# The numerator of a rational function in SBUF instead of PSUM, in the first half of an MoE layer

## The chip, the cores and the metric

The kernel runs on one core of a Trainium2 chip. The metric is the device time of one execution in microseconds. TensorE is called PE, VectorE DVE, ScalarE ACT, GpSimd POOL and SyncE SP, as in the profile. All times of the kernel before are from three timed runs and from one profiled execution.

## What is computed

Three layers follow each other: a pooled attention, a first MoE layer whose activation is a rational function, and a second MoE layer with routing over all tokens. The change is in the activation of the first MoE. Cut to that:

```python
x = attention(q, k, v)               # 4608 tokens x 512
h = x @ w_in                         # 4608 x 2048
P = a[0] + a[1]*h + a[2]*h*h + a[3]*h*h*h
Q = 1.0 + abs(b[0])*abs(h) + abs(b[1])*h*h
g = P / (Q + 1e-06)
x = g @ w_out                        # 4608 x 512, then the second MoE
```

## The kernel before, in words

The 4608 tokens are 18 blocks of 256. The 2048 hidden features are two halves of 1024 (`half` 0 and 1), each of four pieces of 256 (`fp` 0 to 3). The kernel passes over all blocks with the first half, then over all blocks with the second, then does the routing and the second MoE. Attention is computed in the same stretch as the first half: its scores (line 560), transposes (595) and products with v (613 to 616) stand between the matmuls of the first half until about 500 us.

The unit of work is a step: 512 columns of h, either one block times two chunks of 128 features or two blocks times one chunk. There are 72 steps in each half. One step is:

- `mm_h` (line 701): 24 matmuls of 256 columns or 12 of 512 write h into one PSUM bank, `ph`. Each product is done in three parts, high and low halves of both factors.
- `act1`: ACT writes |h| to `ms` (716), a3\*h + a2 to `mw` (717) and |b1|\*|h| + |b0| to `mq` (719). In the tables `mw` and `mq` also appear as `mwq`, since two of the three buffers of each share a tile. DVE multiplies `mw` by h (721) and then computes (mw + a1)\*h (722), which it writes over h in the PSUM bank. POOL multiplies `mq` by `ms` (by way of helper line 353).
- `act2`: ACT takes the logarithm of the denominator (734) and the exponential (736), which gives 1/Q in `mr`. DVE computes the high part of g, `hi` = (numerator + a0)\*`mr` (737), then two more passes (739 and 741) that give the remainder of the division in `mt`. Lines 737 and 741 read the numerator; line 739 reads `mq` and `hi`. POOL multiplies `mt` by `mr` (353), which gives the low part, `lo`. The tiles of `hi` and `lo` are named `mg`, `mgx` or `gd`, and `woh`, `wol` and so on where spent weight tiles are used again.
- `mm_y`: PE multiplies `hi` by the high and low parts of w_out (805, 806) and, later, `lo` by the high part (803). The results of a block gather in two PSUM banks and are read out at 832.

There are eight PSUM banks of 512 columns. `ph`, the output banks, the scores, transposes and v products of attention and the preparation of weights all draw on the same eight. `mw` and `mq` are rings of three, `ms` of two.

The order of the work is not written by hand. Each operation is recorded with an engine, an estimated cost, the keys it reads and those it writes (`op`, and `either` for work that two engines can do). `Order.run` then plans: it walks the engines in the order of planned time, takes the ready operation of lowest priority number, gives a bank to the first user of a `Dyn` from those planned free, and takes it back when the last operation that uses it is planned to end. The result is one fixed instruction order for each engine, in which an instruction waits on semaphores for what it needs. While planned time is under 105 us, the planner also fills planned gaps of PE with matmuls on a tile of zeros (line 339). The bank of `ph` is held from the first matmul of a step to line 741, the last reader of the numerator.

Of the kernel before, what the change touches and what calls it, by code (L numbers as in the profile page):

```python
# [18 lines left out]
ALU = mybir.AluOpType  # L19
# [4 lines left out]
B, H, S, D = 8, 8, 576, 64  # L24
# [7 lines left out]
NB = NT // BLK  # L32
# [266 lines left out]
class Kern:  # L299
# [408 lines left out]
    def act1(self, st):  # L708

        nc, op, i = self.nc, self.op, st["i"]  # L710
        ph = st["ph"]
        hk = [(ph, 0)]
        w, q, s = self.mw[i % 3], self.mq[i % 3], self.ms[i % 2]
        st["w"], st["q"] = ph, q
        N = 2 * BLK
        op("Act", c_act(N), lambda: nc.scalar.activation(s(), ph(), AF.Abs), r=hk, w=[s])  # L716
        op("Act", c_act(N, 0, 2), lambda: nc.scalar.activation(w(), ph(), AF.Identity, scale=self.a3(), bias=self.a2()),
           r=hk + self.sk, w=[w])
        op("Act", c_act(N, 1, 2), lambda: nc.scalar.activation(q(), s(), AF.Identity, scale=self.b1a(), bias=self.b0a()),  # L719
           r=[s] + self.sk, w=[q])  # L720
        op("DVE", c_tt(N), lambda: nc.vector.tensor_tensor(w(), w(), ph(), op=ALU.mult), r=hk, w=[w])
        op("DVE", c_stt(N), lambda: nc.vector.scalar_tensor_tensor(
            ph(), w(), self.a1(), ph(), op0=ALU.add, op1=ALU.mult), r=[w], w=hk)
        self.tt(N, q, q, s, ALU.mult, r=[s], w=[q])

    def act2(self, st):

        nc, op, i = self.nc, self.op, st["i"]
        w, q, r, t = st["w"], st["q"], self.mr[i % len(self.mr)], self.mt[i % MTB]
        hi, lo = g = self.mgl.pop(0)  # L730
        self.mgl.append(g)
        st["hi"], st["lo"] = hi, lo
        N = 2 * BLK
        op("Act", c_act(N, 1, 1), lambda: nc.scalar.activation(r(), q(), AF.Ln, scale=2.0 ** -LNS, bias=self.qcs()),
           r=[q], w=[r])
        op("Act", c_act(N, 1, 1), lambda: nc.scalar.activation(r(), r(), AF.Exp, scale=-1.0, bias=self.nls()), w=[r])
        op("DVE", c_stt(N), lambda: nc.vector.scalar_tensor_tensor(hi(), w(), self.a0(), r(), op0=ALU.add, op1=ALU.mult),  # L737
           r=[(w, 0), r], w=[hi])
        op("DVE", c_stt(N), lambda: nc.vector.scalar_tensor_tensor(t(), q(), self.qc(), hi(), op0=ALU.add, op1=ALU.mult),
           r=[q, hi], w=[t])  # L740
        op("DVE", c_stt(N), lambda: nc.vector.scalar_tensor_tensor(  # L741
            t(), w(), self.a0(), t(), op0=ALU.add, op1=ALU.subtract), r=[(w, 0), self.hring(st)], w=[t])
        self.tt(N, lo, t, r, ALU.mult, r=[t, r], w=[lo])

    def late(self, st):
# [755 lines left out]
    def route(self, k):  # L1501

        nc, V, rop = self.nc, self.nc.vector, self.rop
        D = lambda dur, fn, r=(), w=(), late=False: rop("DVE", dur, fn, r=r, w=w, late=late)
        L = lambda dur, fn, r=(), w=(): D(dur, fn, r, w, k > 0)
        tt, ts, stt = V.tensor_tensor, V.tensor_scalar, V.scalar_tensor_tensor
# [12 lines left out]
        K, BQ, ch, M, S2 = self.K, self.BQ, self.ch, self.M if k else self.Mb, self.S2  # L1519
        cq, cid, ra = self.cq, self.cid, self.ra  # L1520
        rk = lambda x: (self.rp, id(x))
        kk = lambda t, *a: [(t, n) for n in range(*(a or (NB,)))]
        c8 = (ch, 8)
# [28 lines left out]
        def ahead():  # L1552
            cw = lambda t, a, z: t().rearrange("p (g t) -> p g t", t=4)[:, a:z]
            wb = lambda n: self.wrb().unsqueeze(1).unsqueeze(3).to_broadcast([128, n, E, 4])
            for a, z, key in ((0, 8, rk(ch)), (8, 9, c8)):
                if a:
                    D(.1, lambda: ts(ch()[:, 8], self.R()[:, 8], 8.0, None, op0=ALU.is_equal), r=kk(self.R, NB - 2, NB), w=[c8])
                else:
                    D(.34, lambda: V.tensor_reduce(cq()[:, 0:8], K[0]().rearrange("p e g t -> p g t e"), op=ALU.max, axis=AX.X), r=[K[0]], w=[(cq, 0)])
                    own(a, z, key)  # L1560
# [16 lines left out]
        if not last:  # L1577
            if k == 0:
                J, jk = self.small(501, 5)
                D(.07, lambda: V.tensor_copy(J(), self.c("J")), r=[self.rc, *kk(self.R, NB - 2)], w=[jk])  # L1580
                D(.43, lambda: ts(ch()[:, 0:8], self.R()[:, 0:8], 8.0, None, op0=ALU.is_equal), r=kk(self.R, NB - 2), w=[rk(ch)])
                D(.06, lambda: V.memset(self.open8(), 1.0), r=[jk], w=[rk(self.open8)])
            spread(self.kq, BQ)

            def rest():
                if k:
                    D(.34, lambda: V.tensor_reduce(cq()[:, 0:8], K[0]().rearrange("p e g t -> p g t e"), op=ALU.max, axis=AX.X), r=[K[0]], w=[(cq, 0)])
                D(.1, lambda: V.tensor_reduce(cq()[:, 8], K[1]().rearrange("p e t -> p t e"), op=ALU.max, axis=AX.X), r=[rk(K[1])], w=[(cq, 1)])
                if k:
                    D(.37, lambda: tt(self.chw(), ch(), be(self.wrb()), op=ALU.mult), r=[rk(ch), c8, self.wrb], w=[self.chw])  # L1590
                    D(.37, lambda: red(gt(cid), self.chw), r=[self.chw], w=[cid])
                else:
                    own(8, 9, c8)
            so = lambda j: (lambda: self.sole()[:, j:j + 1])
            self.search(D, BQ, 0, QS, NT / E - .5, rest, so(0), True)

            D(.1, lambda: self.tc.mark_branch_hint_location(f"settle{k}", engines=[mybir.EngineType.DVE]), r=[(self.thr, 0)], w=[self.flag])

            T, pt = self.T, Dyn(self.cls_r)
            D(.15, lambda: ts(T()[:, 0:E], self.c("sel"), self.thr()[:, 0:1], None, op0=ALU.mult, op1=ALU.add, accum_out=self.rj()),  # L1600
              r=[self.rc, (self.thr, 0)], w=[(T, 0), self.rj])
            D(.15, lambda: ts(T()[:, E:2 * E], self.c("sel"), so(0)(), None, op0=ALU.mult, op1=ALU.add, accum_out=self.rj()),
              r=[self.rc, (self.sole, 0)], w=[(T, 1), self.rj])
            rop("PE", .2, lambda: nc.tensor.matmul(pt()[:, 0:2 * E], self.c("ones"), T(), start=True, stop=True),
                r=[(T, 0), (T, 1), self.rc], w=[pt])
            D(.08, lambda: V.tensor_reduce(z(0), pt()[:, 0:E], op=ALU.max, axis=AX.X), r=[pt], w=[zk(0)])
            D(.1, lambda: ts(q(0), pt()[:, 0:E], z(0), None, op0=ALU.is_equal, op1=ALU.add, accum_out=so(1)()), r=[pt, zk(0)], w=[qk(0), (self.sole, 1)])
            D(.1, lambda: stt(q(1), pt()[:, E:2 * E], .5, q(0), op0=ALU.is_lt, op1=ALU.mult, accum_out=so(2)()), r=[pt, qk(0)], w=[qk(1), (self.sole, 2)])

            D(.07, lambda: ts(self.flag(), so(1)()[0:1], so(2)()[0:1], 1.5, op0=ALU.add, op1=ALU.is_gt),  # L1610
              r=[(self.sole, 1), (self.sole, 2)], w=[self.flag])
            D(.08, lambda: stt(q(2), pt()[:, 0:E], z(0), wr(), op0=ALU.is_equal, op1=ALU.mult), r=[pt, zk(0), self.rc], w=[qk(2)])
            D(.08, lambda: V.tensor_reduce(z(2), q(2), op=ALU.max, axis=AX.X), r=[qk(2)], w=[zk(2)])
            D(.1, lambda: ts(ra(), cid(), z(2), None, op0=ALU.is_equal), r=[cid, (cid, 0), (cid, 8), zk(2)], w=[rk(ra)])
            D(.1, lambda: stt(M(), f2(cq), z(0), ra(), op0=ALU.is_ge, op1=ALU.mult), r=[(cq, 0), (cq, 1), zk(0), rk(ra)], w=[rk(M)])

            def settle():
                v = V.value_load(self.flag(), min_val=0, max_val=1)
                with self.tc.If(v == 1, label=f"settle{k}"):
                    self.long_way(M)  # L1620
            D(1.5, settle, r=[self.flag, rk(ch), c8, cid, (cid, 0), (cid, 8), self.rc, (self.rp, 501), *[(self.lg, n, j) for n in range(NB) for j in range(4)]],
              w=[rk(M), zk(2), qk(2), K[0], rk(K[1]), K[2], BQ, self.cc, self.chw, (self.chw, 0), (self.chw, 8), self.ge, self.cand, self.nn, self.njunk, self.X, (self.rp, 496), (self.rp, 8), (self.thr, 0), *self.BJ, *[(self.cnt, j) for j in range(4)]])
            if k:
                after()
        else:
            D(.08, lambda: tt(q(2), self.open8(), wr(), op=ALU.mult), r=[rk(self.open8), self.rc], w=[qk(2)])
            D(.08, lambda: V.tensor_reduce(z(2), q(2), op=ALU.max, axis=AX.X), r=[qk(2)], w=[zk(2)])
            L(.1, lambda: ts(M(), self.dead(), 50.0, None, op0=ALU.is_lt), r=[self.dead], w=[rk(M)])
# [355 lines left out]
```

## Time and profile before

| | |
|---|---|
| three timed runs, us | 1498.46, 1502.45, 1506.28 (median 1502.45) |
| profiled execution, us | 1500.95 |
| its span, first to last instruction, us | 1499.2 |
| PE busy in the span | 1451.5 us, 97% |
| DVE, ACT, POOL busy | 72%, 61%, 58% |
| steps of the first half | about 52 us to 605 us |
| attention beside them | until about 500 us |
| steps of the second half | about 602 us to 998 us |

PE's busy time counts a matmul until its last result is out, so short waits between matmuls do not show as idle time. A wait is put down to the instruction whose end came last. "Idle before" of a group is the idle time of the engine just ahead of its instructions.

### The profile page before, as it was taken

The page shows a single profiled execution, that of the slowest core. Times are in us where ns is not written, and L with a number is a line of the kernel's source. Part 1 is how long each engine was busy: PE and PEld are TensorE (multiplying, and loading weights), DVE is VectorE, ACT ScalarE, POOL GpSimd, SP SyncE. Part 2 cuts the span into 40 slices and gives each one's busy share as a digit, 9 for nine tenths or more (in the row PEclk, how much of TensorE's full clock was granted, in tenths as well). Part 3 has the DMA queues.
Part 4 walks back from the last instruction along what each step waited for, and adds up shares of the span by engine and source line. Part 5 has one row for each costly group of instructions (what it writes and reads, how often), then busy time and mean ns, then how long its engine had stood idle before and what let it go on. Part 6 is the DMA issues. An engine that isn't in the chain of part 4 may idle for free. (4 is left out here: it accounts for less than half of the span.)

```text
span 1499.2 us, 27379 instructions
## 1 busy us (share of the span) xinstructions
PE 1451.5 (97%) x9516; PEld 1311.2 (87%) x9516; DVE 1077.9 (72%) x2909; ACT 917.9 (61%) x2203; POOL 877.0 (58%) x809
## 2 busy tenths in 40 slices
PE   8899999999999999999999999998999999999998
PEld 7899978888998999888999899766988988988997
DVE  6898787858678587897777877987878877831220
ACT  5887886868778686765446655842554543542431
POOL 5877887557666465764456554842465654653621
PEclk9999999999999999999999999999899999999999
DMA  6672543232422354531343333013254433433400
GB/s 218 221 238 99 168 144 131 80 113 89 144 99 71 103 153 126 166 82 63 111 113 85 85 97 102 1 47 126 86 173 141 152 113 118 155 121 99 140 26 32
DMA packets 109686, 173.62 MB, mean 116 GB/s; under 512 B 10336, under 2 KB 74208, under 8 KB 109536
## 3 DMA queue, kind: packets, MB, share of 16 engines
q1 hardware_dynamic: 84640, 134.02, 27.7%
q0 software_dynamic: 24896, 37.76, 9.1%
q8 instruction: 75, 1.23, 0.3%
q14 instruction: 75, 0.61, 0.1%
HBM read 122.29 MB, written 49.46 MB: 115 GB/s over the span
## 5 line engine op out<-in xcount | busy, mean ns | idle before, releaser
L701 PE MATMUL pa<-xh,wih 128*128 128x256 f32 (+1 forms) x576 | 202.3, 351 | 2.7 <-ACT ex L573 1.2
L701 PE MATMUL pa<-xh,wil 128*128 128x256 f32 (+1 forms) x576 | 195.4, 339 | 0.2 <-POOL wil L353 0.2
L701 PE MATMUL pa<-xl,wih 128*128 128x256 f32 (+1 forms) x576 | 195.2, 339 | 0.0
L353 POOL TENSOR_TENSOR mwq<-mwq,ms 128x512 f32<-128x512 f32 x96 | 130.2, 1357 | 97.4 <-ACT mwq L719 95.9
L716 ACT ACTIVATE ms<-pa 128x512 f32<-128x512 f32 x144 | 85.9, 596 | 113.0 <-PE pa L701 102.0
L1820 PE MATMUL pa<-yth,w1h 128*128 128x256 f32 (+1 forms) x512 | 146.0, 301 | 0.9 <-issue 0.7
L1820 PE MATMUL pa<-ytl,w1h 128*128 128x256 f32 (+1 forms) x512 | 144.9, 299 | 0.0
L1820 PE MATMUL pa<-yth,w1l 128*128 128x256 f32 (+1 forms) x512 | 144.8, 298 | 0.0
L353 POOL TENSOR_TENSOR mg<-mt,mr 128x512 fp32r<-128x512 f32 x75 | 96.9, 1292 | 61.1 <-DVE mt L741 43.2
L805 PE MATMUL pa<-woh,mg 128*128 128x260 f32 x480 | 125.5, 287 | 4.3 <-DVE mg L737 1.9
L806 PE MATMUL pa<-wol,mg 128*128 128x260 f32 x480 | 123.9, 284 | 0.0
L1873 POOL DMA_INDIRECT out<-ob,ix x40 | 39.0, 976 | 144.0 <-ACT ob L1869 116.0
L701 PEld LDWEIGHTS pa<-xh,wih 128*128 128x128 f32 x576 | 109.8, 191 | 14.5 <-ACT ex L573 2.0
L701 PEld LDWEIGHTS pa<-xh,wil 128*128 128x128 f32 x576 | 109.3, 190 | 13.1 <-POOL wil L353 0.4
L701 PEld LDWEIGHTS pa<-xl,wih 128*128 128x128 f32 x576 | 109.7, 190 | 9.1
L573 ACT ACTIVATE ex<-pa,nm 128x72 f32<-128x72 f32 (+2 forms) x320 | 98.6, 326 | 19.8 <-DVE nm L564 14.3
L741 DVE SCALAR_TENSOR_TENSOR mt<-pa,scal,mt 128x512 f32<-128x512 f32 x144 | 106.9, 743 | 1.3
L1823 ACT ACTIVATE h2h<-pa 128x256 fp32r<-128x256 f32 (+1 forms) x128 | 51.0, 407 | 84.9 <-PE pa L1820 79.5
L1854 PE MATMUL pa<-w2h,h2h 128*128 128x512 f32 x256 | 102.7, 401 | 0.0
L1854 PE MATMUL pa<-w2h,h2l 128*128 128x512 f32 x256 | 100.1, 391 | 0.0
L1828 DVE SCALAR_TENSOR_TENSOR h2l<-pa,h2h 128x256 fp32r<-128x256 f32 x128 | 53.7, 419 | 63.9 <-ACT h2h L1823 59.1
L1820 PEld LDWEIGHTS pa<-yth,w1h 128*128 128x128 f32 x512 | 95.9, 192 | 2.1 <-issue 1.5
(438 smaller groups left out, 4942.4 us busy)
## 6 DMA issues: line engine op xcount, KB each, us to landing
mwq<-in_w SPq DMA_DIRECT2D x42, 512.0 KB, 4.4
wraw<-in_w SPq DMA_DIRECT2D x22, 512.0 KB, 5.0
ya_d<-ya SPq DMA_DIRECT2D x18, 520.0 KB, 2.8
yab<-ya_d SPq DMA_DIRECT2D x18, 520.0 KB
kvraw<-in_kT SPq DMA_DIRECT2D x16, 576.0 KB, 4.2
x_d<-xh SPq DMA_DIRECT2D x18, 512.0 KB, 3.9
x_d<-xl SPq DMA_DIRECT2D x18, 512.0 KB
xh<-x_d POOLq DMA_DIRECT2D x18, 512.0 KB
```

Of the source, the lines that this page charges most:

```text
L353: self.g.either({"Pool": (p_tt(n), lambda: nc.gpsimd.tensor_tensor(out(), x(), y(), op=alu)), "DVE": (c_tt(n), lambda: nc.vector.tensor_te ...
L573: op("Act", c_act(NK, 0, 1, 1), lambda h=h: nc.scalar.activation(e()[:n, h, :], sv()[:, h, :], AF.Exp, bias=nm()[:n, h:h + 1], accum_out=s ...
L701: nc.tensor.matmul(o, w()[:, c, f], x()[:, c].rearrange("p b t -> p (b t)") if two else x()[:, c, :], start=c == 0 and k == 0, stop=c == 3 ...
L716: op("Act", c_act(N), lambda: nc.scalar.activation(s(), ph(), AF.Abs), r=hk, w=[s])
L741: op("DVE", c_stt(N), lambda: nc.vector.scalar_tensor_tensor(t(), w(), self.a0(), t(), op0=ALU.add, op1=ALU.subtract), r=[(w, 0), self.hri ...
L805: nc.tensor.matmul(o, hi()[:, f], w(woh), start=first, stop=False)
L806: nc.tensor.matmul(o, hi()[:, f], w(wol), start=False, stop=False)
L1820: nc.tensor.matmul(ps()[:, 0:n], w()[:, c, fs], x()[:, c, :], start=i == 0, stop=i == 11)
L1823: fop("Act", c_act(n), lambda hh=hh, t=t, n=n, ps=ps: nc.scalar.activation(hh()[:, t], ps()[:, 0:n], AF.Relu), r=[ps], w=[(hh, half)])
L1828: fop("DVE", c_stt(t1 - t0), lambda hh=hh, o=o, o0=o0, ps=ps, t0=t0, t1=t1, half=half: nc.vector.scalar_tensor_tensor(o()[:, o0:o0 + t1 - ...
L1854: nc.tensor.matmul(ps(), x()[:, t], w()[:, f % 2, :], start=f == 0 and i == 0, stop=False)
L1873: fop("Pool", 1.05, lambda ob=ob, c=c, n=n: nc.gpsimd.indirect_dma_start(out=self.out, out_offset=bass.IndirectOffsetOnAxis(ap=ix()[:n, c: ...
```

## The change

In steps of the first half (`half` 0), line 722 writes the numerator into `mw`, the SBUF tile that already holds its first factor, and no longer over h in PSUM. `st["w"]`, which `act2` reads in lines 737 and 741 (740 and 744 in the changed file), is then `mw`. Steps of the second half are as before. The keys follow: line 722 of the first half reads the bank and writes `mw`, and the readers name `mw` too. Two more keys are added in the routing, which order an instruction behind another that uses the same small region of PSUM.

```diff
         op("DVE", c_stt(N), lambda: nc.vector.scalar_tensor_tensor(
-            ph(), w(), self.a1(), ph(), op0=ALU.add, op1=ALU.mult), r=[w], w=hk)
+            (ph if st["half"] else w)(), w(), self.a1(), ph(), op0=ALU.add, op1=ALU.mult),
+           r=[w] if st["half"] else hk, w=hk if st["half"] else [w])
+        if st["half"] == 0:
+            st["w"] = w
         self.tt(N, q, q, s, ALU.mult, r=[s], w=[q])
...
         op("DVE", c_stt(N), lambda: nc.vector.scalar_tensor_tensor(hi(), w(), self.a0(), r(), op0=ALU.add, op1=ALU.mult),
-           r=[(w, 0), r], w=[hi])
+           r=[(w, 0), w, r], w=[hi])
...
         op("DVE", c_stt(N), lambda: nc.vector.scalar_tensor_tensor(
-            t(), w(), self.a0(), t(), op0=ALU.add, op1=ALU.subtract), r=[(w, 0), self.hring(st)], w=[t])
+            t(), w(), self.a0(), t(), op0=ALU.add, op1=ALU.subtract), r=[(w, 0), w, self.hring(st)], w=[t])
...
-                    D(.1, lambda: ts(ch()[:, 8], self.R()[:, 8], 8.0, None, op0=ALU.is_equal), r=kk(self.R, NB - 2, NB), w=[c8])
+                    D(.1, lambda: ts(ch()[:, 8], self.R()[:, 8], 8.0, None, op0=ALU.is_equal), r=[(self.rp, 501), *kk(self.R, NB - 2, NB)], w=[c8])
...
-                D(.43, lambda: ts(ch()[:, 0:8], self.R()[:, 0:8], 8.0, None, op0=ALU.is_equal), r=kk(self.R, NB - 2), w=[rk(ch)])
+                D(.43, lambda: ts(ch()[:, 0:8], self.R()[:, 0:8], 8.0, None, op0=ALU.is_equal), r=[jk, *kk(self.R, NB - 2)], w=[rk(ch)])
```

The costs that the planner uses do not change, but its plan does, since a bank comes free at line 722 of a step and no longer at line 741. The number of instructions is the same on every engine but PE, where 217 of the zero matmuls of line 339 stand in place of 212. Buffers are numbered in the rows below (`pa7` is a PSUM bank).

DVE at the first step, in the kernel before, from line 721 to the weight preparation of line 453:

```order
L721 TENSOR_TENSOR mwq0_744<-mwq0_744,pa7_274 128x512
L722 SCALAR_TENSOR_TENSOR pa7_274<-mwq0_744,scal_93,pa7_274 128x512
L517 TENSOR_REDUCE ks_133<-kvraw_98 128x144
L627 SCALAR_TENSOR_TENSOR xl0_362<-pa0_130,xh0_353 128x2x256
L627 SCALAR_TENSOR_TENSOR xl1_809<-pa3_197,xh1_795 128x2x64
L578 TENSOR_SCALAR sm2_400,junk_218<-sm2_400 96x4
L564 TENSOR_REDUCE nm2_385<-pa5_233 128x4
L579 RECIPROCAL sm2_400<-sm2_400 96x4
L599 TENSOR_TENSOR ptl1_495<-pa6_270,pth1_468 128x2x64
L602 TENSOR_TENSOR pth1_468<-pa6_270,pth1_468 32x64
L453 TENSOR_TENSOR wol1_659<-pa0_130,woh1_628 128x2x4
L737 SCALAR_TENSOR_TENSOR mg0_865<-pa7_274,scal_93,mr0_835 128x512
```

The same place in the changed kernel:

```order
L721 TENSOR_TENSOR mwq0_744<-mwq0_744,pa7_274 128x512
L722 SCALAR_TENSOR_TENSOR mwq0_744<-mwq0_744,scal_93,pa7_274 128x512
L517 TENSOR_REDUCE ks_133<-kvraw_98 128x144
L627 SCALAR_TENSOR_TENSOR xl0_362<-pa0_130,xh0_353 128x2x256
L627 SCALAR_TENSOR_TENSOR xl1_813<-pa3_197,xh1_795 128x2x64
L453 TENSOR_TENSOR wol1_659<-pa7_274,woh1_628 128x2x4
```

The numerator goes to `mwq0`, bank `pa7` is given to the weight preparation at once, and that preparation moves ahead of five small instructions of attention.

PE about halfway through the attention stretch, in the kernel before: the end of the v product of attention, then the last quarter of `mm_h` of a step, then the low and high parts of `mm_y` of older steps. `mgx0` is `hi` of the step with piece `wih2` and its first chunk.

```order
L615 MATMUL pa3_197<-ptl1_495,vmh1_124 128x192
L616 MATMUL pa3_197<-pth1_468,vmh1_124 128x192
L701 MATMUL pa0_130<-xh0_353,wih2_976 128x512
L701 MATMUL pa0_130<-xl0_362,wih2_976 128x512
L701 MATMUL pa0_130<-xh0_353,wil2_1009 128x512
L560 MATMUL pa6_270<-kbd1_112,qraw1_104 128x144 x2
L803 MATMUL pa4_231<-woh1_628,mg0_865 128x260
L803 MATMUL pa5_233<-woh1_628,mg0_865 128x260
L805 MATMUL pa4_231<-woh2_1169,mgx0_2652 128x260
```

The same place in the changed kernel (lines 803 and 805 are 806 and 808 there):

```order
L615 MATMUL pa4_231<-ptl1_495,vmh1_124 128x192
L616 MATMUL pa4_231<-pth1_468,vmh1_124 128x192
L701 MATMUL pa5_233<-xh0_353,wih3_1460 128x512
L701 MATMUL pa5_233<-xl0_362,wih3_1460 128x512
L701 MATMUL pa5_233<-xh0_353,wil3_1473 128x512
L806 MATMUL pa3_197<-woh1_628,mg0_873 128x260
L806 MATMUL pa0_130<-woh1_628,mg0_873 128x260
L808 MATMUL pa3_197<-woh2_1145,mgx0_2674 128x260
```

Ahead of the same `mm_y` PE has now done `mm_h` of one more step: the matmuls there use piece `wih3`, where they used `wih2`. From the tenth step of the second half to its end PE's order is the same in both. In the last steps of the first half and in the second MoE single pieces of weight preparation, transposes and routing stand some places earlier or later.

## Rows read from the trace of the kernel before

**Rows 1.** The page, part 1: busy us (share of the span) xinstructions.

```profile
PE 1451.5 (97%) x9516; PEld 1311.2 (87%) x9516; DVE 1077.9 (72%) x2909; ACT 917.9 (61%) x2203; POOL 877.0 (58%) x809
```

**Rows 2.** Windows: stretch, length, PE, PEld, DVE, ACT, POOL busy, PEclk, DMA share, GB/s.

```profile
50.00:150.00 100.00, 94.02 (x785) 91.55 (x784) 88.27 (x186) 87.04 (x264) 77.09 (x86) 1.00 0.53 172
150.00:500.00 350.00, 337.05 (x2278) 305.04 (x2277) 261.74 (x593) 275.69 (x848) 239.77 (x277) 0.99 0.35 113
500.00:605.00 105.00, 104.87 (x887) 104.66 (x886) 85.00 (x143) 76.54 (x156) 60.26 (x54) 1.00 0.47 137
605.00:1000.00 395.00, 386.44 (x2380) 342.24 (x2379) 324.86 (x605) 243.40 (x391) 228.81 (x186) 0.99 0.31 87
1000.00:1499.20 499.20, 484.80 (x2857) 429.19 (x2856) 285.63 (x1297) 203.67 (x428) 238.76 (x157) 0.99 0.35 113
```

**Rows 3.** Waits of PE, 50 to 500 us: who <- whom: us total, times, longest.

```profile
PE pa L803 <- POOL mg L353: 3.0, 3, 1.6
PE pa L339 <- ACT ex L573: 2.2, 2, 1.4
PE pa L805 <- DVE mg L737: 1.9, 2, 1.6
PE pa L560 <- DVE mt L741: 1.9, 3, 0.7
PE pa L805 <- DVE mt L741: 1.4, 2, 0.9
PE pa L701 <- ACT ex L573: 1.2, 1, 1.2
PE pa L339 <- DVE xl L627: 1.0, 1, 1.0
PE pa L805 <- DVE xl L627: 0.8, 1, 0.8
...
PE pa L595 <- DVE mt L741: 0.3, 1, 0.3
```

**Rows 4.** Timeline of one step on ACT and DVE: start, length, engine, line, what.

```profile
126.53 0.60 ACT L716 ACTIVATE ms<-pa 128x512 f32<-128x512 f32 x1 [1.71 <-PE pa L701]
...
129.11 0.76 DVE L722 SCALAR_TENSOR_TENSOR pa<-mwq,scal,pa 128x512 f32<-128x512 f32 x1
132.33 0.75 DVE L737 SCALAR_TENSOR_TENSOR mg<-pa,scal,mr 128x512 fp32r<-128x512 f32 x1 [2.46 <-ACT mr L736]
...
135.43 0.74 DVE L741 SCALAR_TENSOR_TENSOR mt<-pa,scal,mt 128x512 f32<-128x512 f32 x1
```

**Rows 5.** Lines 722, 737, 739, 741 on DVE, 50 to 605 us: ns minimum/median/maximum.

```profile
L722 DVE SCALAR_TENSOR_TENSOR pa<-mwq,scal,pa x48: 721/748/757, 54.5 to 597.4; 128x512 f32<-128x512 f32 x48
L737 DVE SCALAR_TENSOR_TENSOR mg<-pa,scal,mr x52: 714/750/754, 60.7 to 604.7; 128x512 fp32r<-128x512 f32 x52
L739 DVE SCALAR_TENSOR_TENSOR mt<-mwq,scal,mg x35: 740/814/2414, 62.0 to 601.6; 128x512 f32<-128x512 f32 x35
L741 DVE SCALAR_TENSOR_TENSOR mt<-pa,scal,mt x71: 720/742/752, 64.9 to 602.9; 128x512 f32<-128x512 f32 x71
```

**Rows 6.** Timelines of DVE and POOL: one instruction of line 739 and POOL's beside it.

```profile
144.76 2.41 DVE L739 SCALAR_TENSOR_TENSOR mt<-mwq,scal,mg 128x512 f32<-128x512 f32 x1
144.19 2.43 POOL L353 TENSOR_TENSOR ya<-ya,yap 128x1040 f32<-128x1040 f32 x1
```

**Rows 7.** Windows of line 739 alone: stretch, length, DVE busy (instructions), PEclk, DMA share, GB/s.

```profile
50.00:150.00 100.00, 14.75 (x11) 1.00 0.53 172
150.00:500.00 350.00, 44.62 (x45) 0.99 0.35 113
500.00:605.00 105.00, 15.94 (x15) 1.00 0.47 137
```

**Rows 8.** POOL's product for lo, 50 to 605 us: busy, mean ns | idle before.

```profile
L353 POOL TENSOR_TENSOR mg<-mt,mr 128x512 fp32r<-128x512 f32 x51 | 65.8, 1289 | 43.5 <-DVE mt L741 30.9 <-DVE sm L579 3.0 <-ACT woh L452 2.4
```

**Rows 9.** A window just behind a wait of PE for lo, columns as in rows 2.

```profile
241.00:245.00 4.00, 4.00 (x18) 3.62 (x18) 2.51 (x6) 2.64 (x11) 3.80 (x5) 0.57 0.30 86
```

## The prediction, made before the changed kernel ran

> **What bounds the kernel now.** I read the page first: PE is busy 97% of the span [rows 1], so a change elsewhere counts only by what PE waits for. The windows by stretch say where that is [rows 2]. While attention runs beside the first half, PE stands idle 6.0 us of 100 (50 to 150 us) and 13.0 us of 350 (150 to 500). In the rest of the first half (500 to 605) it is idle for 0.1 us, although DVE is busy 85.0 of 105. So the change, which touches only the 72 steps of the first half, can win at most what PE loses from 50 to 500: 19 us of idle time, and whatever hides in the tails of matmuls. DVE is busy 88.3 of 100 us from 50 to 150, ACT 87.0. This is the one stretch in which an engine other than PE is nearly full.
>
> The table of PE's waits in that stretch [rows 3] has two kinds. In the first, PE wants a PSUM bank that is not free: the score, transpose, `mm_y` and zero matmuls (560, 595, 805, 339) that wait for the end of line 741, for the exponentials of the scores (573) or for the low part of x (627). In the second PE wants data: `lo` from POOL (803 behind `mg` of line 353, 3.0 us) and `hi` from DVE (805 behind line 737, 1.9 us).
>
> **What the change takes away.** The bank of h is read last at line 722 and no longer at line 741. In the step of [rows 4] that is 129.87 in place of 136.17, so 6.3 us earlier of the 9.6 us from the first read of h (126.53) on. With 56 steps in 450 us, a step each 8.0 us, this is about 0.8 bank of eight free at any time.
> The waits that end with line 741 go: 1.9 + 1.4 + 0.3 = 3.6 us [rows 3]. The other bank waits shown there, 2.2 + 1.2 + 1.0 + 0.8 = 5.2 us, end with other readers. 0.8 bank more relieves these in part; their ends are 0 and 5.2, and I take 3. Together 6.6 us.
>
> **What moves.** PE's order now runs a step further ahead in places: in the second pair of order rows `mm_h` of piece `wih3` is done before the `mm_y` that had `wih2` ahead of it. Where this is so, `hi` and `lo` have more matmuls in front of them before PE wants them. DVE's order gives the bank on at once, to weight preparation in the first pair. In the second MoE the order moves too, by single instructions. PE is idle there 14.4 us of 499 [rows 2] on routing and loads that are not part of this change, and I expect no more than 3 us either way, the size of single waits in rows 3, and take 0.
>
> **What it adds.** No instruction is new. Line 722 keeps one operand in PSUM and one in SBUF and gets the form of lines 737 and 741 of before, and those took 742 to 750 ns where 722 took 748 [rows 5]: 0. But lines 737 and 741 now read two tiles of SBUF, the form that only line 739 had. This is the price of the change. Lines 737 and 741 never took more than 754 ns. Line 739 takes 740 at best and 2414 at worst [rows 5]. At its worst POOL was in a tensor_tensor from 144.19 to 146.62, and line 739, begun at 144.76, ended at 147.17, 0.55 us after POOL [rows 6]. So the form with two SBUF tensors waits until POOL's instruction is over, and the form with a PSUM operand does not.
>
> The size is in the windows of line 739 alone [rows 7], against 0.745 us of an undisturbed one. From 50 to 150: 14.75 / 11 = 1.34, so 0.60 more. From 150 to 500: 44.62 / 45 = 0.99, so 0.25 more. From 500 to 605: 15.94 / 15 = 1.06, so 0.32 more. If both lines paid the full price, DVE would get 2 x (11 x 0.60 + 45 x 0.25 + 15 x 0.32) = 45 us; the other end is 0, and less than 0 is excluded since the shortest line 739 (740) is no shorter than the median line 741 (742). I take half, 22 us. The three instructions of a step stand close together (737 at 132.33, 741 at 135.43 [rows 4]) and a product of POOL lasts 1.29 us [rows 8], so one that line 737 has waited out is not waited for again by line 739.
>
> [...]
>
> **What of this reaches PE.** From 50 to 150, half the price is 11 x 0.60 = 6.6 us on DVE, which had 11.7 us free. Much of that free time lies where DVE waits for ACT, so I let half of it through: 3 us. From 150 to 500, DVE goes from 262 to 273 of 350 us and the further run-ahead covers most steps; `hi` comes 0.12 us later and `lo` 0.25, and I let 1 us through. If the run-ahead fails, each of 45 steps pays 0.25, 11 us. From 500 to 605 the order has no more room than before, and 15 x 0.32 = 4.8 us fall on DVE; PE had no idle time there, so there was some slack: 1.5 us. Who waits behind the new delays: on DVE the reductions, transposes and `xl` of attention, on POOL everything behind `lo`. POOL's queue already stood 30.9 us before `lo` for line 741 [rows 8], and POOL's product for the next step's denominator stands behind it. Sum: 5.5 us, with ends 0 and 22 (6.6 + 11 + 4.8).
>
> [...]
>
> **The sum.** -6.6 + 5.5 = -1.1; 0.6 us more may be won in tails of matmuls that show no idle time. That makes about -2 on the profiled execution's own 1500.95 (span 1499.2 and 1.75 around it), so 1499. The median of the three runs is 1502.45, by which it would be 1500.5; the runs lie from 1498.5 to 1506.3. A measurement of this kernel tells about 0.5%, 7.5 us, from no change.
>
> **The rivals.**
> Faster, 1485: banks are what PE lacks all over the attention stretch. All bank waits go (8.8 us) and so do, by the longer run-ahead, the waits for `lo` and `hi` (4.9) and the two stretches of slow clock (3.4), while the port costs 1.5: -15.6. For it: PE loses nearly all its time where attention competes for banks and almost none from 500 on. Against it: DVE and ACT are at 88 and 87% from 50 to 150.
> Slower, 1516: POOL's port. All three lines pay the full price of line 739, 45 us more DVE time. From 50 to 150 DVE would have 88.3 + 13.2 = 101.5 us of work in 100, and `lo` comes 0.5 us later in each step, 72 x 0.25 = 18 us if half reaches PE. With 3.6 us of bank waits gone: +15. It decides from the point at which the means of lines 737 and 741 reach that of line 739, about 1.06 us, and the run-ahead has no room left. [...] For it: the wait is certain in kind. Against it: shared waits, and slack that PE has shown from 500 on.
> No relief, 1504: the planner hands the free bank on at once (it does so with `pa7`), so PE waits as often for other owners. Then 3.6 us go at most and 5.5 come, +2 to +3.
>
> **How the numbers follow.** Forecast, 1491 to 1507 around 1499: 0.42. Faster rival: 0.30. Slower rival: 0.20. No relief: 0.08. Of the forecast's own 0.42 about 0.04 lies below 1495 and 0.03 above 1510, so faster by over 0.5% is 0.34, slower 0.23, within 0.5% 0.43. The range 1483 to 1516 leaves out about half of each outer rival's own spread, some 0.1 at each end.
>
> **What would show it.** Right: no PE wait names line 744 (741 before) between 50 and 500 us; lines 740 and 744 spread up to 2 us and average 0.85 to 1.0; line 722 stays at 0.75; DVE gains 15 to 30 us in the first half; the stretch from 500 to 605 gets 1 to 2 us longer. Wrong: the two lines stay at 0.75, so the port costs nothing (then 1494 or less); or they average over 1.1 and PE waits for `mg` grow past 15 us (then the slower rival); or the time moves in the second half or the second MoE, where nothing was priced.

## The result and the profile after

The changed kernel takes 1518.87 us (median of 4, 1516.71 to 1519.13) against 1501.84 (4 runs, 1498.46 to 1506.28): a ratio of 1.0108, interval [1.0080, 1.0137]. It is 17 us slower, and the forecast of 1499 and its range to 1516 are both missed. The profiled execution has a span of 1517.4 us. In it lines 737, 739, 741, 803 and 805 of the kernel before are lines 740, 742, 744, 806 and 808.

The page's first part, which answers to [rows 1] (busy us, share of the span, instructions):

```profile
PE 1451.4 (96%) x9521; PEld 1306.0 (86%) x9521; DVE 1118.7 (74%) x2909; ACT 920.6 (61%) x2203; POOL 900.3 (59%) x809
```

DVE runs as many instructions as before and is busy 40.8 us longer. PE's busy time is the same, so what was added to the span (18.2 us in the profiled executions) is idle time of PE. The windows by stretch, which answer to [rows 2] (stretch, length; PE, PEld, DVE, ACT, POOL busy; PEclk, DMA share, GB/s), say where:

```profile
50.00:150.00 100.00, 93.28 (x776) 90.54 (x775) 89.81 (x185) 87.26 (x260) 78.00 (x88) 1.00 0.50 167
150.00:500.00 350.00, 327.30 (x2189) 292.34 (x2188) 287.51 (x578) 269.48 (x825) 250.67 (x270) 1.00 0.35 113
500.00:605.00 105.00, 100.05 (x832) 98.97 (x832) 83.73 (x136) 70.78 (x158) 59.24 (x53) 1.00 0.40 121
605.00:1000.00 395.00, 386.80 (x2470) 346.61 (x2469) 323.76 (x599) 250.26 (x404) 229.46 (x183) 1.00 0.31 90
1000.00:1499.20 499.20, 489.17 (x2876) 432.05 (x2875) 301.24 (x1328) 210.00 (x440) 247.83 (x164) 0.99 0.34 113
```

PE's busy time falls by 0.7 us from 50 to 150, by 9.8 from 150 to 500 and by 4.8 from 500 to 605: 15.3 us. Another 2.0 us lie in the first 50 us (44.27 to 42.25), ahead of the steps. Behind the first half nothing is lost: from 605 to 1000 us PE is as busy as before (386.80 against 386.44), and from the end of the last step of the second half to the end of the kernel it is 500.2 us, where it was 501.2. So neither the second MoE nor the two added keys of the routing took the time. From 50 to 605 us DVE is busy 26 us longer, and fewer steps are done by then.

The three lines on DVE, in order 740, 742 and 744, each over 50 to 624 us, which is the whole rest of the first half here (stretch, length, DVE busy with the instructions, PEclk, DMA share, GB/s; they answer to [rows 7]):

```profile
50.00:624.00 574.00, 78.82 (x71) 1.00 0.39 124
50.00:624.00 574.00, 73.50 (x71) 1.00 0.39 124
50.00:624.00 574.00, 70.39 (x70) 1.00 0.39 124
```

Against 0.745 us for each, as before, lines 740 and 744 wait 78.82 - 71 x 0.745 = 25.9 and 70.39 - 70 x 0.745 = 18.2 us, together 44.1 where there was nothing (lines 737 and 741 average 0.746 and 0.743 us in the kernel before). Line 742 waits 73.50 - 71 x 0.745 = 20.6; line 739 waited 75.31 - 52.9 = 22.4 (the sum of [rows 7]). So the price of the form with two SBUF operands is here the full one, 44 of the 45 us that the prediction gave as its upper end, and the line that paid before goes on paying. Line 722, with one operand in PSUM and its output now in SBUF, stays at 740 ns.

What a wait looks like, from the timelines of DVE and POOL (start, length, engine, line, what; idle time before in brackets). First DVE, then POOL beside it:

```profile
548.02 0.94 DVE L740 SCALAR_TENSOR_TENSOR mg<-mwq,scal,mr 128x512 fp32r<-128x512 f32 x1
...
549.48 1.19 DVE L742 SCALAR_TENSOR_TENSOR mt<-mwq,scal,mg 128x512 f32<-128x512 f32 x1
550.59 0.73 DVE L722 SCALAR_TENSOR_TENSOR mwq<-mwq,scal,pa 128x512 f32<-128x512 f32 x1
551.25 1.12 DVE L744 SCALAR_TENSOR_TENSOR mt<-mwq,scal,mt 128x512 f32<-128x512 f32 x1
```

```profile
547.11 1.30 POOL L353 TENSOR_TENSOR mwq<-mwq,ms 128x512 f32<-128x512 f32 x1
548.37 1.74 POOL L353 TENSOR_TENSOR wilb<-wf,wihb 128x512 fp32r<-128x512 f32 x1
550.30 1.52 POOL L353 TENSOR_TENSOR wilb<-wf,wihb 128x512 fp32r<-128x512 f32 x1 [0.19 <-ACT wihb L359]
```

POOL's three instructions end at 548.41, 550.11 and 551.82; lines 740, 742 and 744 end at 548.96, 550.67 and 552.37, each 0.55 or 0.56 us behind one of them. One step pays three times, to three different instructions of POOL. Line 722, inside the same 1.52 us product, takes 0.73. The example is no exception: of the three lines' instructions in the first half 98 took over 0.85 us, and 97 of these ended 0.54 to 0.57 us behind an instruction of POOL.

The waits of PE from 50 to 620 us, which answer to [rows 3] (who <- whom: us in total, times, longest):

```profile
PE pa L806 <- POOL mg L353: 6.0, 8, 1.3
PE pa L560 <- DVE xl L627: 4.7, 3, 3.2
PE pa L808 <- DVE mg L740: 3.8, 4, 2.1
PE pa L701 <- DVE xl L627: 3.1, 4, 1.1
...
PE pa L339 <- DVE mw L722: 1.4, 1, 1.4
PE pa L808 <- DVE mw L722: 1.2, 1, 1.2
```

No wait names line 744, as predicted: the bank is free from line 722 on. But `lo` is waited for 6.0 us in place of 3.0, `hi` 3.8 in place of 1.9, and banks are waited for that line 627 (`xl` of attention) still reads, 8.8 in place of 2.8 us over all its rows. Line 627 itself is no longer than before (median 550 ns, before 558). It stands behind the longer lines on DVE, as ahead of the longest of these waits, 3.19 us, at whose end PE starts line 560 at 217.58:

```profile
210.44 1.79 DVE L740 SCALAR_TENSOR_TENSOR mgx<-mwq,scal,mr 128x512 fp32r<-128x512 f32 x1
212.15 1.77 DVE L740 SCALAR_TENSOR_TENSOR mgx<-mw,scal,mr 128x512 fp32r<-128x512 f32 x1
213.85 1.49 DVE L742 SCALAR_TENSOR_TENSOR mt<-mwq,scal,mgx 128x512 f32<-128x512 f32 x1
...
217.25 0.28 DVE L627 SCALAR_TENSOR_TENSOR xl<-pa,xh 128x128 fp32r<-128x128 f32 x1
```

Line 722, the new last reader of h's bank, ends 5.3 us of waits (five rows) where line 741 ended 3.6. Over 50 to 605 us PE's waits in this table add to 33.4 us (40 of them), against 17.8 (25) before.

### The profile page after: what moved, and what is told of

Read it like the earlier page. It is cut to its first block, busy times and chain, and to the rows that moved or that the text cites. A ratio compares the mean times of both kernels' runs of the same rounds, so it can differ in the third digit from the quotient of the medians.

```text
span 1517.4 us, 27369 instructions
## 1 busy us (share of the span) xinstructions
PE 1451.4 (96%) x9521; PEld 1306.0 (86%) x9521; DVE 1118.7 (74%) x2909; ACT 920.6 (61%) x2203; POOL 900.3 (59%) x809
## 5 line engine op out<-in xcount | busy, mean ns | idle before, releaser
L353 POOL TENSOR_TENSOR mwq<-mwq,ms 128x512 f32<-128x512 f32 x96 | 133.9, 1395 | 91.3 <-ACT mwq L719 91.0
L353 POOL TENSOR_TENSOR mg<-mt,mr 128x512 fp32r<-128x512 f32 x75 | 100.8, 1344 | 75.8 <-DVE mt L744 49.5
L573 ACT ACTIVATE ex<-pa,nm 128x72 f32<-128x72 f32 (+2 forms) x320 | 99.0, 329 | 26.6 <-DVE nm L564 18.1
L808 PEld LDWEIGHTS pa<-woh,mg 128*128 128x128 f32 x480 | 90.4, 188 | 9.0 <-DVE mg L740 5.1
L353 POOL TENSOR_TENSOR en<-ex,sm 128x256 f32<-128x256 f32 (+5 forms) x160 | 85.9, 559 | 20.5 <-DVE sm L579 5.3
```

What stands on the lines that cost most here:

```text
L353: self.g.either({"Pool": (p_tt(n), lambda: nc.gpsimd.tensor_tensor(out(), x(), y(), op=alu)), "DVE": (c_tt(n), lambda: nc.vector.tensor_te ...
L573: op("Act", c_act(NK, 0, 1, 1), lambda h=h: nc.scalar.activation(e()[:n, h, :], sv()[:, h, :], AF.Exp, bias=nm()[:n, h:h + 1], accum_out=s ...
L808: nc.tensor.matmul(o, hi()[:, f], w(woh), start=first, stop=False)
```

## The experiments

Theory **PORT**: the loss is the DVE time that lines 740 and 744 wait for POOL, and it reaches PE because the fixed orders leave it little room. Rival **ORDER**: the loss comes from PE's changed order beside attention, and these waits cost little. PORT, and "the port" in the prediction, are only names for these waits: the traces show when DVE waits for POOL, and not what in the chip makes it wait. In every comparison below the kernel before ran on the same chip (medians 1501.91, 1501.75 and 1502.90).

**The numerator in SBUF, but the bank kept.** The bank is now held to line 744, so this is the price without the early bank:

```
- r=[(w, 0), w, r], w=[hi])
+ r=[(w, 0), w, r, *([] if st["half"] else [(st["ph"], 0)])], w=[hi])
  (and the same on line 744)
```

> The numerator is in SBUF as in the changed kernel, but the plan still holds the bank of h to the last reader of the numerator, so PE's order is nearly the one of the kernel before (746 of 9507 instructions stand elsewhere, bank names aside). Theory PORT (lines 737 and 741, 740 and 744 in the changed kernel, wait for POOL's instruction when both operands are in SBUF, and that costs the time): the two lines average 1.0 to 1.15 us in the first half, time 1515 to 1530, the same as the changed kernel or above it by what the early bank gave back. Theory ORDER (the new plan that the free bank brings costs the time): the lines may be long, but the time is 1498 to 1506 as before.

Measured: 1531.48 us (1530.12 to 1535.03), 1.0196 [1.0174, 1.0218]. The lines 740, 742 and 744 there:

```profile
50.00:635.00 585.00, 73.72 (x71) 0.98 0.38 121
50.00:635.00 585.00, 79.53 (x71) 0.98 0.38 121
50.00:635.00 585.00, 66.53 (x71) 0.98 0.38 121
```

That is just above the range expected by PORT, 1515 to 1530. With PE's order near that of before, the price is there without the gain: 29.6 us, though lines 740 and 744 wait 34.4 us, less than in the changed kernel. ORDER falls; the changed kernel's order is 12.5 us better than this one. Not all of that is banks: PE's granted clock here is 0.97 and 0.98 in the first two stretches, where the changed kernel has 1.00 (the columns are those of [rows 2]):

```profile
50.00:150.00 100.00, 92.53 (x742) 88.99 (x741) 88.93 (x179) 83.39 (x253) 77.03 (x85) 0.97 0.49 158
150.00:500.00 350.00, 322.37 (x2137) 287.97 (x2136) 275.29 (x567) 261.97 (x812) 241.84 (x265) 0.98 0.35 112
```

**Plain delay on DVE, everything else as before.** Columns of lines 737 and 739 are computed once more ahead of the row, in the form with a PSUM operand, in which no wait for POOL shows (no added row takes more than 10 ns above the mean of its kind: 513 ns for 288 columns, 426 for 208, 245 for 32; the whole rows of lines 737 and 741 in these kernels average 751 and 744 ns). The first kernel repeats 288 and 208 columns, the second 32 and 32:

```
+ def more(o, n):
+     if st["half"] == 0:
+         nc.vector.scalar_tensor_tensor(o()[:, 0:n], w()[:, 0:n], self.a0(), r()[:, 0:n], ...)
  line 737: more(hi, 288) ahead of the row;  line 739: more(t, 208)
```

> The kernel before, order unchanged, with more DVE work in the first half: 288 columns of line 737 are computed once more just ahead of it (0.38 us), and 208 columns just ahead of line 739 (0.28 us), both with an operand in PSUM, so about 0.65 us in each of 72 steps, 46 us of DVE as in the changed kernel, but evenly spread and without the port. Theory PORT as plain DVE delay: PE passes on about as much as in the changed kernel, 1515 to 1530. If it needs the uneven waits, or POOL's longer instructions, 1503 to 1510. ORDER: under 1506, since the order is the one of before.

> The kernel before, with a smaller delay on DVE: in each of the 72 first-half steps 32 columns of line 737 and 32 of line 739 are computed once more ahead of the whole row, in the form with a PSUM operand. By what the rows of 288 (513 ns) and 208 columns (426 ns) took, some 0.23 us each, 0.47 us a step, 34 us, less some 8 us that line 739 waits less for POOL: about 26 us more of DVE. SLACK (the prediction's step: DVE has room, a quarter of such a delay reaches PE, and only the larger delay overran the room): +5 to +8, 1507 to 1510. PROPORTION (the order leaves no room, 0.7 of every delay reaches the end): +16 to +20, 1518 to 1522.

Measured: 1537.61 us (1533.75 to 1540.42), +35.7, and 1519.99 us (1517.37 to 1521.80), +17.1. The first parts of their pages:

```profile
PE 1462.5 (95%) x9516; PEld 1312.8 (85%) x9516; DVE 1128.7 (73%) x3053; ACT 920.3 (60%) x2203; POOL 872.1 (57%) x809
```

```profile
PE 1456.6 (96%) x9516; PEld 1310.7 (86%) x9516; DVE 1099.8 (72%) x3053; ACT 920.2 (61%) x2203; POOL 874.5 (58%) x809
```

DVE is busy 50.8 and 21.9 us longer than before, so 0.70 and 0.78 of a DVE microsecond comes out at the end. The first was expected by PORT at 1515 to 1530 and came out above it; the second is in the range of PROPORTION. The smaller delay passes no less than the larger: there is no room that only a large delay overruns. This is the step of the prediction that let 5.5 of 22 us through. One thing differs from the changed kernel: here the bank of h is still held to the delayed line 741 (744 in these files). In the first kernel the three largest waits that name it add to 10.8 us, where all of them made 3.6 before, so a part of this delay reaches PE by way of that bank.

**POOL's products taken away.** In the first half POOL's two products of each step become a product of 8 columns and memsets, so POOL hardly reads SBUF for them. These products are left out of the computation. With three memsets a step's piece took longer than the product (1.49 against 1.30 us), so both were run again with two:

```
+ G.tensor_tensor(out()[:, 0:8], x()[:, 0:8], y()[:, 0:8], op=ALU.mult)
+ for c in (8, 8, 344):        # then (8, 8)
+     G.memset(out()[:, c:512], v)
```

> The changed kernel with the same order on PE, DVE and ACT; in the first half POOL's two products of a step (denominator and lo) are left out, all but 8 columns, and three memsets of about the same length stand in their place, which write SBUF and do not read it. Theory PORT: the three DVE lines fall to 0.75 to 0.90 us on average and the time to 1480 to 1500. Theory ORDER: the time stays at 1512 to 1522 whatever the lines do.

> The kernel before with the same replacement of POOL's two products in the first half (left out all but 8 columns, memsets in their place). PORT: line 739 falls from 1.06 us to 0.75 to 0.90 and the time by 3 to 10 us, to 1491 to 1499. The difference to the run with the changed kernel's order is then what the early bank is worth without the port: 0 to 10 us in favour of the changed kernel. ORDER: the changed kernel's order stays 15 us or more behind this one.

> As the changed kernel whose POOL products in the first half are replaced by an 8-column product and memsets (POOL's products are left out, so that part of the result is not computed), with two memsets in place of three, so that POOL's work is no longer than its products were. With three it was 1506.5. If POOL's longer chain cost it time: 1498 to 1503, below the kernel before, which would show what the early bank is worth with half the price. If what remains is the DVE waits that the memsets still cause: 1505 to 1507.

> The kernel before with the same replacement in POOL (its products in the first half are left out) with two memsets, the comparison for the changed kernel with the same. With three it was 1503.5. If POOL's chain is what held it: 1494 to 1499. If the order and the planned starts hold it: 1502 to 1504. The difference to the changed kernel with the same replacement is the price that is left (some 20 us of DVE) less the early bank: within +-4 if the bank is worth 12 us.

Measured with three memsets: the changed kernel 1506.47 (1504.29 to 1509.16), the kernel before 1503.51 (1501.42 to 1506.51). The first lies in neither theory's range, the second above its own. With two: 1494.17 (1493.99 to 1495.39), 0.9938 [0.9921, 0.9954], and 1495.67 (1492.93 to 1497.12), 0.9942 [0.9923, 0.9961]. The first parts of the pages of these last two:

```profile
PE 1446.9 (97%) x9521; PEld 1305.1 (87%) x9521; DVE 1083.9 (73%) x2909; ACT 917.0 (61%) x2203; POOL 880.0 (59%) x1097
```

```profile
PE 1446.1 (97%) x9516; PEld 1305.6 (87%) x9516; DVE 1069.0 (72%) x2909; ACT 917.2 (61%) x2203; POOL 856.1 (57%) x1097
```

Without those reads the changed kernel loses 34.8 us of DVE time, and its distance to the kernel before goes from +17.0 to -8.7. The kernel before loses 8.9 us of DVE time and 7.2 at the end. These two falls are not the worth of POOL's reads alone, since POOL's own work changed too. With three memsets POOL is busy 14.8 and 13.8 us longer than in the two kernels with products (915.1 and 890.8 us), with two 20.3 and 20.9 us shorter. That step of 35 us cost 13.3 and 8.8 us at the end, each measured from the kernel before on its chip. On a straight line between the two versions (an estimate), POOL's work left as long as it was, the changed kernel would come out 18.1 us earlier for it and the kernel before 1.9.

What doesn't hang on this is the comparison of the two kernels with the same replacement. The changed one is 17.0 us behind with the products and 3.0 behind with three memsets; with two it is 1.5 ahead, and their runs overlap. So 14 us or more of the 17 go with POOL's reads. That is PORT, taken away rather than added.

What is left in the changed order with two memsets, 14.9 us more of DVE than in the order of before, costs nothing there (1494.17 against 1495.67). That fits an early bank that pays for it.

**Only the last 15 steps, and only the first 57.** The new placement where step `i` is at least 57 (behind attention), and where it is below:

```
- (ph if st["half"] else w)()
+ (ph if st["half"] or i < 57 else w)()        # the other kernel: i >= 57
  (and the same in r=, w= and st["w"])
```

> The changed placement only in the last 15 of the 72 steps (500 to 605 us), where PE had been idle 0.1 us and wants no bank; the order of PE stays nearly that of before. PORT (the loss is DVE time, since lines 740 and 744 now wait for POOL): 15 steps x 0.64 us = 9.6 us more of DVE, of which the changed kernel lost about 5 here, so about 1507 us, +4 to +7. ORDER (the loss comes from PE's changed order beside attention): no loss here, 1502 +- 2.

> The changed placement only in the first 57 steps (up to 500 us), where attention takes banks and the early bank can pay. PORT: 57 x 0.64 = 36 us more of DVE, less what the early bank gives back; the changed kernel had lost about 13 by there, so +11 to +15, 1513 to 1517. ORDER: the whole loss sits here, +15 to +18. Together with the last 15 steps alone the two differences should add to the 17 us of the whole change.

Measured: 1508.47 (1506.30 to 1510.85), 1.0042 [1.0029, 1.0055], and 1513.23 (1512.68 to 1514.16), 1.0074 [1.0057, 1.0091]: +6.7 and +11.5, together 18.2 for the 17.0 of the whole. Two windows, of the first kernel from 500 to 605 us and of the second from 50 to 500 (columns as in [rows 2]):

```profile
500.00:605.00 105.00, 100.68 (x832) 99.87 (x831) 81.23 (x127) 70.31 (x145) 58.15 (x49) 0.98 0.44 129
```

```profile
50.00:500.00 450.00, 421.69 (x2957) 383.93 (x2956) 376.11 (x761) 355.69 (x1082) 329.75 (x356) 0.99 0.39 125
```

Both lie in the ranges expected by PORT. Behind attention PE falls from 104.87 to 100.68 us of 105, although DVE is busy only 81.23 of them. The first kernel's idle time there begins after 525 us, and attention's last product with v is at 524.7, so attention no longer takes banks. Lines 740 and 744 wait 7.1 us there (15.25 us in 15 and 13.47 in 14 instructions), and 6.7 come out at the end. In the second kernel PE is busy 421.69 us of the attention stretch where it was 431.07 (94.02 + 337.05). DVE is 32.4 us longer busy (1110.3 us on its page) for 11.5 at the end, 0.35. The early bank gives something back there, and the last 15 steps show nothing of the kind.

**The planner told the price.** The changed kernel with +0.37, +0.30 and +0.28 us on its three lines' costs in the first half, and the kernel before with +0.30 on line 739:

> The changed kernel, with the planner told what its three lines took in the first half (line 740 +0.37 us, 742 +0.30, 744 +0.28). PORT with a price that passes whatever the order: 1516 to 1521, as the changed kernel. If much of the loss is that the plan places attention's DVE work and PE's matmuls as though the steps were 0.95 us shorter: 1505 to 1513.

> The kernel before, with the planner told +0.30 us for line 739 in the first half, as line 739 took, and with the two added orderings in the routing that the changed kernel has. If a plan with truer durations wins PE time: 1495 to 1500. If, as the changed kernel told its prices (1528), true durations make a worse plan: 1503 to 1510.

Measured: 1527.96 (1526.70 to 1530.18) and 1505.03 (1501.93 to 1509.62), 1.0014 [0.9998, 1.0030]. So a plan with the true durations doesn't win the time back; the changed kernel's gets 9 us worse, which neither theory expected and which stays unexplained, and that of before is within its interval of no change. I had it first without the two orderings in the routing that the diff adds:

> The kernel before, with the planner told what line 739 took in the first half (+0.30 us). If a plan with true durations wins PE time: 1495 to 1500. If the plan's order is not what loses time, or a longer row only moves work elsewhere: 1502 +- 3.

It took 1506.07 (1500.58 to 1510.62), but its routing changed with the order, so it is not read further. No kernel that computes all came out below the kernel before.

## Why the prediction was wrong

**The price: the step "I take half, 22 us" failed.** The reason given was that a POOL product which line 737 has waited out is not waited for again by line 739. The 548 us example shows the opposite, and the sums do too: line 742 still waits 20.6 us, and lines 740 and 744 wait 44.1 on top: 44 us where the sum took 22. POOL has other work between (attention's products, weight preparation), and each line of a step meets another instruction. The upper end, 45 us, was right. Its shape was not: from 150 to 500 us line 740 waits most, 51.89 us in 44 instructions, 0.43 us each above 0.745 against 0.25 in the estimate, and from 50 to 150 least, 0.24 against 0.60:

```profile
50.00:150.00 100.00, 10.83 (x11) 1.00 0.50 167
150.00:500.00 350.00, 51.89 (x44) 1.00 0.35 113
500.00:624.00 124.00, 16.10 (x16) 1.00 0.40 122
```

That lines 737 and 741 would wait as line 739 did was drawn from line 739 alone [rows 5, 6], and the changed kernel shows it: 44.1 us for 141 instructions of lines 740 and 744, 0.31 us each, where line 739 waited 22.4 us in 71, 0.32 each, in the kernel before. (The prediction calls the shortest line 739, 740 ns, no shorter than the median line 741, 742 ns; it is 2 ns shorter, and nothing hangs on it.)

**The way to PE: the step "I let 1 us through" failed most.** Of 22 us the sum passed 5.5, a quarter, for DVE's free time and the longer run-ahead. Delay that stands on DVE alone passed at 0.70 to 0.78, in both sizes. Idle time in a window was taken as room, but of DVE's 120 us of idle time from 50 to 605 us in the kernel before, at least 99 are waits for ACT or PE. A delay of a row then moves what comes behind it; that this is why so much passes is argued, and the share that passed is measured. From 500 to 605 I read PE's 0.1 us of idle time as slack: 1.5 us forecast, 4.8 lost. The run-ahead that was to cover 150 to 500 us did not; the prediction's own price if it failed, 11 us, is near the 9.8 that PE lost there, but by luck: lines 740 and 744 waited 30.5 us in that stretch, and what the early bank gave back is in the 9.8. Nor did I see who would wait: I named `hi`, `lo` and attention's tiles, and the largest growth is in the banks that line 627 gives back late (2.8 to 8.8 us): what the early bank of h won was paid for in part with later banks of attention.

**The early bank: the sign and the place were right, the size stays open.** At 0.70 to 0.83 of the added DVE time (the kernel with the bank kept gives 0.83), the changed kernel's 40.8 us would cost 28.6 to 33.9; it lost 17.0, so 11.6 to 16.9 came back. The pair without POOL's products gives 11.9 to 13.9 (14.9 us of DVE, and 1.5 us better), the pair with the bank kept and not kept 16 to 17. In the kernels with added delay a longer row also holds h's bank longer, so this counts more than the 6.6 us of waits that the prediction counted. Part of it may be clock. The changed kernel's runs have a mean granted clock of 0.994, those with the bank kept and with the larger delay 0.988, those of before 0.991 to 0.992, and if all of the time went with the clock, 0.001 of 1500 us would be 1.5 us. With all of that taken out, of the delays too (0.58 to 0.78 then passes), about 3 to 11 us are left. The prediction's 6.6 us lie inside this. Its sum has nothing for the clock; that is not borne out in the mean, but single runs overlap. No run shows the 3.4 us that the faster rival adds for two stretches of slow clock. What the traces show from 50 to 605 us is a granted clock of 0.57 twice in the kernel before, over 241 to 245 us [rows 9] and 346.5 to 350.5, each behind a wait of PE of 1.6 us, and of 0.58 once in the changed kernel, over 219 to 223 us, behind its wait of 3.19 us. What those stretches cost at the end was not measured. Whether fewer pauses of PE caused the better clock, or it fell so by chance, these runs don't settle.

**What held.** Nothing waits for line 744; line 722 keeps its 0.74 us; the second half doesn't move; the form with two SBUF operands waits for POOL (of lines 740, 742 and 744 in the first half 98 of 212 instructions took over 0.85 us), and in the form with one in PSUM no wait shows (line 722 averages 740 ns). Of the signs given, DVE's gain of 15 to 30 us came out at 40.8, and the means of lines 740 and 744, 1.11 and 1.01 us, lie above the 0.85 to 1.0 of the forecast and at the 1.06 from which the slower rival was to decide. That rival came nearest, 1516, with the full price, 18 of its 45 us reaching PE and 3.6 back. More passed and more came back, so that it came near is in part luck: the two errors nearly cancelled. Its sign, 15 us of PE waits for `mg`, did not show: there are 9.8, and 8.8 of waits for attention's banks beside them.

## What to carry to other kernels

When an operand of a DVE instruction moves from PSUM to SBUF, look at what a line that already has that form pays for POOL in the same stretch, and charge every such line the full price (here 0.32 us an instruction on line 739 before, and 0.31 on average on the two lines that were changed). Don't count an engine's idle share as room when another engine's order is fixed against it: put a plain delay of known size there, and see what part comes out at the end (here 0.7 to 0.8 for both sizes tried, 0.6 to 0.8 if the clock's part is taken out). Here the early bank gave something back only where other work wanted the bank; where nothing did, in the last 15 steps, the same edit was pure cost, 6.7 us. And when work is left out to take a cause away, see that what stands in its place takes as long: here 35 us of POOL's time moved the end by 9 to 13 us.

## What the runs showed of the hardware

**One DVE instruction took 3.78 us, over three POOL instructions in a row.** It is one of line 740 in the changed kernel. The timelines of DVE and POOL:

```profile
352.63 3.78 DVE L740 SCALAR_TENSOR_TENSOR mg<-mw,scal,mr 128x512 fp32r<-128x512 f32 x1
```

```profile
351.84 1.84 POOL L534 TENSOR_TENSOR kvraw<-kvraw 128x768 f32<-128x768 f32 x1
353.64 1.27 POOL L353 TENSOR_TENSOR mwq<-mwq,ms 128x512 f32<-128x512 f32 x1
354.88 0.99 POOL L534 TENSOR_TENSOR kvraw<-kvraw 128x384 f32<-128x384 f32 x1
```

It ended at 356.41, 0.54 us behind the third of them (355.87). The three POOL instructions follow each other without a gap, and line 740 did not end in between.

**Beside POOL's memsets no wait of DVE shows.** In the changed kernel with two memsets, 52 instructions of the three lines (754, 756 and 758 there) began inside a memset, and they took 0.746 us on average; 74 began inside a POOL product of other parts of the kernel and took 0.42 us more on average. One of the first kind, from the timelines of DVE and POOL:

```profile
299.67 0.75 DVE L754 SCALAR_TENSOR_TENSOR mg<-mwq,scal,mr 128x512 fp32r<-128x512 f32 x1 [0.36 <-ACT mr L753]
```

```profile
298.96 1.09 POOL L364 MEMSET mgx<- 128x504 f32 x2
```

**POOL's product for `lo` got longer too.** It went from 1289 ns [rows 8] to 1359 on average, in the groups of POOL from 50 to 620 us:

```profile
L353 POOL TENSOR_TENSOR mg<-mt,mr 128x512 fp32r<-128x512 f32 x50 | 68.0, 1359 | 57.4 <-DVE mt L744 35.9 <-DVE sm L578 9.4 <-DVE sm L579 4.1
```

The growth sits in few of them: of this product's 70 instructions there, of the group above and of that for `mgx`, 11 began inside one of the three lines (0.1 us or more before its end) and took 1.68 us on average, and the other 59 took 1.29. In the kernel before none of 73 began inside line 739, and they took 1.29. So in the changed kernel each is longer beside the other, and POOL's wait for line 744 grew from 30.9 to 35.9 us with it.
